# Which tokens of the second layer are put off: a block in four of 32 groups in place of the last 8 groups whole

## The chip, the cores and the metric

The kernel runs on one core of one Trainium2 chip. The metric is device time in microseconds, from runs of the whole kernel; smaller is better. The engines are PE (matmuls; PEld is its load of weights), DVE, ACT and POOL; SP issues transfers.

## The reference, cut to what matters

```
X = fft(fft(x, axis=1), axis=2).real          # 8 x 3072 x 256, as 24576 tokens
h = (X @ w1) * (X @ w2) @ w3                  # 256 -> 1024 -> 1024
y = h @ w_out                                 # 1024 -> 256
logits = y @ w_gate                           # 8 experts
...                                           # greedy routing, 3072 tokens an expert
out[mask] = relu(y[mask] @ w1[e]) @ w2[e]
```

`w3`, `w_out` and `w_gate` are multiplied out ahead, so the second layer is one product with a matrix `W` of 1024 x 264: 256 columns give `y`, the last 8 the logits.

## The kernel before, in words

**Stage A** (`stage_a`, line 280) walks over 8 batches, 2 sets of frequencies and 3 columns of tokens: 48 groups of 512 tokens, numbered 0 to 47. Each group has 8 steps, one for each slice `f` of 128 of the 1024 hidden features; the list `steps` (line 957) has 384 of them, and the loop at line 967 runs it.

A step has a front and a back. `front` (line 813) makes the two first products by 13 matmuls (12 of 256 columns at lines 220 to 222 through `mm3`, one of 512 at line 836). ACT copies one half (840), DVE makes sum, difference (842, 843) and their product `qs` (859), ACT rounds that to float32r as `ah` (853), and POOL makes the rest `al = qs - ah` (854). `back` (line 896) runs three steps later (`LAG = 3`) and multiplies with `W`: `l2` (line 792) takes 4 blocks of 128 tokens, each as the weights of three matmuls of 264 columns (ah with both parts of `W`, then al with the high part), at lines 800, 801 and 804, and at 796 through `mm3` in the last slice. After slice 7, ACT copies the four accumulators, POOL stores logits in `L` and token numbers (`store`, line 915), and SP writes the rows to `xs_d`.

Between steps the loop also folds the input of the next batch on POOL (`fold_batch`, line 456, three loads `xt` of 1 MB a batch) and makes the transforms of the next set (`dft_a`, `dft_b`; the tables of the latter are cut by `tb`, line 316). `middle` (line 921) makes the column that the symmetry leaves over, in the last set of the last batch.

**What is put off.** The last 8 groups (`ASIDE = 8`, line 29; `number` at line 861 counts them 0 to 7) don't run `l2` in stage A. Routing needs every logit, so `logits` (line 876) makes these alone: the 16 columns of the gate in `W`, high and low part side by side (`gates`, line 1003), are the weights, and the 512 tokens move:

```
nc.tensor.matmul(a[:2 * E], gates[0][:, f], ahl[0], start=f == 0, ...)
nc.tensor.matmul(a[:E], gates[0][:, f, :E], ahl[1], start=False, ...)
```

After the last slice ACT copies the 16 rows, four matmuls turn them (line 890) and DVE puts them in `L` (894). `ah` and `al` of seven of these groups go to `away` in DRAM by SP (856, 857); those of the last one (`KEPT = 1`) are written straight to the places of two tables that are done with (`put`, line 868).

**Stage B** (`stage_b`, line 1018) routes the tokens and runs the experts. Its first routing is a chain of small operations that leaves PE idle; the generator `putoff` (line 1334) fills those gaps with the second layer of the tokens put off: 8 lots of 8 slices, 12 matmuls of 256 columns each (line 1371).

**Order.** PE, DVE, ACT and POOL run in the order that the program writes (`manual_schedule(engines=ALL)`, `ALL` on line 203 names these four; SP's order is not written by hand). `later(n, fn)` and `due()` put a piece n steps off.

Of the kernel before, what the change touches and what calls it, by code (L numbers as in the profile page):

```python
# [224 lines left out]
@with_exitstack  # L225
def body(ctx, tc, I, out, nb=NB, dbg=None):
    nc = tc.nc
    vec, act, pool = nc.vector, nc.scalar, nc.gpsimd
    dram = ctx.enter_context(tc.tile_pool(name="dram", bufs=1, space=bass.MemoryType.DRAM))
    xs_d = dram.tile([N, XW], F32, name="xs_d")  # L230
    ed = dram.tile([2, NB, 3, 768], F32R, name="ed")
    em = dram.tile([3, NB], F32R, name="em")
    sp_d = dram.tile([8, NB, 128], F32R, name="sp_d")
    md = dram.tile([NB, D], F32, name="md")
    away = dram.tile([max(ASIDE - KEPT, 1), NF, 128, 2, 512], F32R, name="away")

    keep = ctx.enter_context(tc.tile_pool(name="keep", bufs=1))
    own = ctx.enter_context(tc.tile_pool(name="own", bufs=1))
    L = keep.tile([128, E, NT], F32, name="L")
    small = keep.tile([128, SMALL.shape[1]], F32, name="small")  # L240
    sc = {k: small[:, o:o + w] for k, (o, w) in SOFF.items()}

    aside = 0 if dbg else ASIDE
    putoff = {}
    if dbg == "A":
        nc.vector.memset(L, 0.0)
    if dbg == "B":
        nc.sync.dma_start(L, I["Lin"])
        nc.sync.dma_start(small, I["small"])
        xs_d = I["xs"]  # L250
        k = loader(K_ns(locals()))
    else:
        k = loader(K_ns(locals()))
        stage_a(tc, I, nb, k)
    if dbg == "A":
        nt = 24 * nb
        nc.sync.dma_start(out["L"], L)
        nc.sync.dma_start(out["xs"][:nt * 128], xs_d[:nt * 128])
        return
    stage_b(tc, I, out, k)  # L260
# [19 lines left out]
def stage_a(ctx, tc, I, nb, k):  # L280
# [7 lines left out]
    def accs(i):  # L288
        return psum.tile([128, 512], F32, tag=f"acc{i}", name=f"acc{i}", bufs=1)
# [523 lines left out]
    def front(g):  # L813
        b, st, q, f = g
        c = slice(q * 256, (q + 1) * 256)
        (Eh, El), (Oh, Ol) = EOs[(b, st)]
        if f == 0:
            if g == steps[0]:
                extras(g)
            e3t[0] = e3t[1]  # L820
        if f == 4:
            i = steps.index(g) + 4
            if i < len(steps):
                extras(steps[i])
        e3 = e3t[0]
        n = number(g)
        spill = 0 <= n < k.aside - KEPT

        qs = work.tile([128, 512], F32, name="qs", bufs=4)
        ab = qs.rearrange("p (s c) -> p s c", s=2)  # L830

        us, ue = l1(), l1()
        for w in range(2):
            o = us[:, w * 256:(w + 1) * 256]
            mm3(nc, o, SW[0][:, w, fs(f)], SW[1][:, w, fs(f)], Oh[:, c], Ol[:, c], w == 0, True)
        nc.tensor.matmul(ue, ew[:, fs(f)], e3.rearrange("p w c -> p (w c)"), start=True, stop=False, skip_group_check=True)  # L836
        for w in range(2):
            o = ue[:, w * 256:(w + 1) * 256]
            mm3(nc, o, CW[0][:, w, fs(f)], CW[1][:, w, fs(f)], Eh[:, c], El[:, c], False, True)
        act.activation(qs, us, AF.Copy)  # L840
        pm = work.tile([128, 2, 2, 256], F32, name="pm", bufs=1)
        vec.tensor_tensor(pm[:, 0].rearrange("p w c -> p (w c)"), ue, qs, op=ALU.add)  # L842
        vec.tensor_tensor(pm[:, 1].rearrange("p w c -> p (w c)"), ue, qs, op=ALU.subtract)  # L843
        if n < 0 or spill:
            ah = work.tile([128, 512], F32R, name="ah", bufs=3)
            al = work.tile([128, 512], F32R, name="al", bufs=3)
        else:
            ah, al = put(f)
        if n >= 0:
            k.putoff[n, f] = None if spill else (ah, al)  # L850

        def parts():
            act.activation(ah, qs, AF.Copy)  # L853
            (vec if n == k.aside - 1 and f in LAST else pool).tensor_tensor(al, qs, ah, op=ALU.subtract)  # L854
            if spill:
                cp(nc.sync, k.away[n, f, :, 0], ah)
                cp(nc.sync, k.away[n, f, :, 1], al)

        return ah, al, parts, lambda: vec.tensor_tensor(ab, pm[:, :, 0], pm[:, :, 1], op=ALU.mult)  # L859

# [7 lines left out]
    def put(f):  # L868

        key, t = (("tabA", tabA), ("tabB", tabs["B"]))[f // 4]  # L870
        if key not in places:
            places[key] = own.tile(list(t.shape), F32R, name=key).rearrange("p a b -> p (a b)")
        at = f % 4 * 1024
        return places[key][:, at:at + 512], places[key][:, at + 512:at + 1024]

    def logits(n, f, ahl, j0):

        if f == 0:
            acct[0] = accs(n % 4)
        a = acct[0]  # L880
        nc.tensor.matmul(a[:2 * E], gates[0][:, f], ahl[0], start=f == 0, stop=False, skip_group_check=True)
        nc.tensor.matmul(a[:E], gates[0][:, f, :E], ahl[1], start=False, stop=f == NF - 1, skip_group_check=True)
        if f < NF - 1:
            return
        lt = work.tile([2 * E, 512], F32, name="xo")
        u = accs((n + 2) % 4)[:, :4 * E].rearrange("p (i e) -> p i e", i=4)

        def turn():
            for i in range(4):
                nc.tensor.matmul(u[:, i], lt[:, i * 128:(i + 1) * 128], sc["twice"][:2 * E], start=i == 0, stop=i == 3, skip_group_check=True)  # L890

        later(1, lambda: act.activation(lt, a[:2 * E], AF.Copy))
        later(2, turn)
        later(3, lambda: vec.tensor_copy(L[:, :, j0:j0 + 4].rearrange("p e j -> p j e"), u))

    def back(g, ahl):
        b, st, q, f = g
        n = number(g)
        if n >= 0:
            logits(n, f, ahl, (b * 6 + st * 3 + q) * 4)  # L900
            return
        if f == 0:
            acct[0] = [accs(i) for i in range(4)]
        acc = acct[0]
        l2(acc, ahl[0], ahl[1], f, 4)
        if f < NF - 1:
            return
        j0 = (b * 6 + st * 3 + q) * 4
        for h in range(2):
            xo = work.tile([128, 2, 264], F32, name="xo")  # L910
            act.activation(xo[:, 0], acc[2 * h][:, :264], AF.Copy)
            (vec.tensor_copy(xo[:, 1], acc[2 * h + 1][:, :264]) if EV else act.activation(xo[:, 1], acc[2 * h + 1][:, :264], AF.Copy))
            later(1, lambda xo=xo, j=j0 + 2 * h: store(xo, j))

    def store(xo, j):
        pool.tensor_copy(L[:, :, j:j + 2].rearrange("p e j -> p j e"), xo[:, :, D:])
        pool.tensor_copy(xo[:, :, D:D + 4], sc["tok"][:, j:j + 2, None].to_broadcast([128, 2, 4]))
        nc.sync.dma_start(k.xs_d[j * 128:(j + 2) * 128].rearrange("(i p) d -> p i d", p=128), xo[:, :, :XW])


    def middle():
# [25 lines left out]
        for b in range(nb):  # L947
            p, j = DUP[b]
            if b == nb - 1:
                yield  # L950
            nc.sync.dma_start(L[p:p + 1, :, j], xo[b:b + 1, D:])
            if j // 4 < nb * 6 - k.aside:
                nc.sync.dma_start(k.xs_d[j * 128 + p:j * 128 + p + 1, :D], xo[b:b + 1, :D])
        yield

# [62 lines left out]
def stage_b(ctx, tc, I, out, k):  # L1018
# [315 lines left out]
    def putoff():  # L1334
# [11 lines left out]
            ready.append(k.putoff[n, f])  # L1346

        def finish(n, acc):
            j0 = NT - 4 * ASIDE + 4 * n
            for i in range(2):  # L1350
                xo = ex.tile([128, 2, XW], F32, name="xo")
                act.activation(xo[:, :, :D], acc[i], AF.Copy)
                j = j0 + 2 * i
                pool.tensor_copy(xo[:, :, D:], k.sc["tok"][:, j:j + 2, None].to_broadcast([128, 2, 4]))
                nc.sync.dma_start(xrows[j * 128:(j + 2) * 128].rearrange("(i p) d -> p i d", p=128), xo)
            for b, (p, j) in enumerate(DUP):
                if j0 <= j < j0 + 4:
# [58 lines left out]
    def later(n, fn):  # L1416
        late.append([n, fn])
# [228 lines left out]
```

## Time and profile before

| | us |
|---|---|
| median of 3 runs | 2814.88 (2814.3 to 2817.58) |
| the profiled execution | 2810.5 |
| its span, first to last instruction | 2808.7 |
| PE busy | 2674.4 (95%) |
| DVE, POOL, ACT busy | 2135.4, 1518.0, 1323.0 |

The profile is of one execution. Its time of 2810.5 us lies 4.4 below the median of the runs; the span within it is 1.8 shorter. Busy times are those of one engine each and overlap. Matmuls are pipelined: a matmul's duration is longer than the time to the next one's start, and it is the latter that adds up.

### The profile page before, as it was taken

The numbers are of one execution on the slowest core, as the hardware profiler recorded it, in microseconds if no ns is written. First come the engines' busy times: TensorE is split into PE (matmuls) and PEld (weight loads), VectorE is DVE, ScalarE is ACT, GpSimd is POOL, SyncE is SP. The second block draws the span as 40 slices with busy tenths as digits, with TensorE's granted clock in tenths as the row PEclk, the third lists the DMA queues.
The fourth block names the chain that finished last, engine by engine and source line by source line (L and its number), as shares of the span: only waits on it lengthen the run. The fifth ranks groups of instructions, "written<-read, shape, count | busy, mean of one in ns | idle before, by whom it ended". The sixth has DMA issues, their size and how long they took to land.

```text
span 2808.7 us, 51817 instructions
## 1 busy us (share of the span) xinstructions
PE 2674.4 (95%) x19903; PEld 2454.0 (87%) x19903; DVE 2135.4 (76%) x3795; ACT 1323.0 (47%) x2383; POOL 1518.0 (54%) x1529
## 2 busy tenths in 40 slices
PE   4999999999999999999996999989999999999998
PEld 2899999999999999987796788878888888889997
DVE  8788787978878797888877888788787878862222
ACT  2344444444444444444363747466573746543332
POOL 7295775939577593964304244353535435363532
PEclk8999999999999999999997999999999999999999
DMA  6410110101011011145394112211212122121211
GB/s 232 133 54 32 39 46 24 54 32 54 32 39 47 24 52 34 52 162 200 128 338 154 36 65 54 69 50 46 76 43 73 48 67 54 43 68 43 76 46 35
DMA packets 104705, 207.32 MB, mean 74 GB/s; under 512 B 35178, under 2 KB 60442, under 8 KB 99338
## 3 DMA queue, kind: packets, MB, share of 16 engines
q1 hardware_dynamic: 81000, 131.02, 13.7%
q0 software_dynamic: 22224, 72.58, 8.0%
q8 instruction: 157, 2.57, 0.4%
q14 instruction: 90, 0.74, 0.1%
q10 hardware_dynamic: 1234, 0.41, 0.1%
HBM read 118.15 MB, written 80.28 MB: 71 GB/s over the span
## 4 chain that ended last, share of the span: by engine, by line
PE 73%; DVE 17%; ACT 3%; issue 2%; DMA 1%; POOL 1%; another core or an unknown queue 0%; DVEq 0%; ACTq 0%; POOLq 0%; SPq 0%
PE yp L1483 13%; PE l L220 7%; PE l L222 7%; PE l L221 7%; PE acc L804 5%; PE acc L800 5%; PE acc L801 5%; PE hp L220 4%; PE hp L221 4%; PE hp L222 4%; DVE oR L1086 4%; PE l L836 3%; DVE W L1466 2%; ACT ja L1081 2%; PE hp L1371 2%
## 5 line engine op out<-in xcount | busy, mean ns | idle before, releaser
L854 POOL TENSOR_TENSOR al<-qs,ah 128x512 fp32r<-128x512 f32 x376 | 513.4, 1365 | 406.2 <-ACT ah L853 311.4
L1483 PE MATMUL yp<-FA,W 128*128 128x256 f32 x3040 | 622.0, 286 | 17.8 <-DVE W L1466 8.4
L1483 PEld LDWEIGHTS yp<-FA,W 128*128 128x128 f32 x3040 | 497.8, 190 | 44.6 <-ACT yo L1489 14.9
L859 DVE TENSOR_TENSOR qs<-pm 128x512 f32<-128x512 f32 x384 | 427.4, 1113 | 41.2 <-DVE pm L843 1.8
L853 ACT ACTIVATE ah<-qs 128x512 fp32r<-128x512 f32 x376 | 237.2, 631 | 358.2 <-DVE qs L859 317.7
L1466 DVE SCALAR_TENSOR_TENSOR W<-hp,W 128x512 fp32r<-128x512 f32 x336 | 230.1, 687 | 227.0 <-ACT W L1462 205.0
L1483 PE MATMUL yp<-FB,W 128*128 128x256 f32 x1520 | 388.0, 282 | 0.0
L842 DVE TENSOR_TENSOR pm<-l,qs 128x512 f32<-128x512 f32 x384 | 264.7, 689 | 149.4 <-PE l L222 116.2
L840 ACT ACTIVATE qs<-l 128x512 f32<-128x512 f32 x384 | 227.0, 591 | 235.3 <-PE l L222 220.0
L220 PE MATMUL hp<-tabA,tabB 128*128 128x512 f32 x768 | 319.5, 416 | 0.9 <-ACT tabA L1432 0.9
L1493 POOL DMA_INDIRECT out_dram<-yo,oi x188 | 191.7, 1020 | 231.3 <-DMA out_dram<-yo,oi 217.8
L1462 ACT ACTIVATE W<-hp 128x512 fp32r<-128x512 f32 x336 | 197.2, 593 | 251.6 <-PE hp L222 232.7
L221 PE MATMUL hp<-tabA,tabB 128*128 128x512 f32 x768 | 304.0, 396 | 6.0 <-DVE tabA L1436 6.0
L1483 PEld LDWEIGHTS yp<-FB,W 128*128 128x128 f32 x1520 | 287.9, 189 | 14.3
L800 PE MATMUL acc<-W,ah 128*128 128x264 f32 x1120 | 283.6, 284 | 0.0
L801 PE MATMUL acc<-W,ah 128*128 128x264 f32 x1120 | 283.3, 284 | 0.0
L1086 DVE TENSOR_SCALAR_CACHE_REDUCE oR<-oR,nx 128x1536 uint16<-128x1536 uint16 x196 | 281.4, 1459 | 0.0
L843 DVE TENSOR_TENSOR pm<-l,qs 128x512 f32<-128x512 f32 x384 | 261.2, 680 | 0.0
L1407 POOL DMA_INDIRECT xt<-xs_d,idx x192 | 194.9, 1015 | 109.1 <-issue 49.9
L1457 POOL TENSOR_TENSOR W<-xo,W 128x512 fp32r<-128x512 f32 x48 | 66.6, 1387 | 336.8 <-ACT W L1455 321.1
L222 PE MATMUL hp<-tabA,tabB 128*128 128x512 f32 x624 | 246.7, 395 | 0.0
L220 PE MATMUL l<-eo,SW 128*128 128x256 f32 x768 | 220.7, 287 | 0.0
(350 smaller groups left out, 6930.4 us busy)
## 6 DMA issues: line engine op xcount, KB each, us to landing
xs_d<-xo SPq DMA_DIRECT2D x96, 260.0 KB
xt<-in_xg_dram SPq DMA_DIRECT2D x24, 1024.0 KB
away<-ah SPq DMA_DIRECT2D x56, 256.0 KB
away<-al SPq DMA_DIRECT2D x56, 256.0 KB
yo<-away SPq DMA_DIRECT2D x28, 512.0 KB
raw<-in_w3t_dram SPq DMA_DIRECT2D x16, 512.0 KB
FA<-away SPq DMA_DIRECT2D x14, 512.0 KB
FB<-away SPq DMA_DIRECT2D x14, 512.0 KB
```

The lines of the kernel that those rows point to most:

```text
L220: nc.tensor.matmul(out, ah, bh, start=start, stop=False, skip_group_check=True)
L221: nc.tensor.matmul(out, ah, bl, start=False, stop=False, skip_group_check=True)
L222: nc.tensor.matmul(out, al, bh, start=False, stop=stop, skip_group_check=True)
L800: nc.tensor.matmul(acc[i][:, :264], ah[:, a], W[0][:, f], start=f == 0, stop=False, skip_group_check=True)
L801: nc.tensor.matmul(acc[i][:, :264], ah[:, a], W[1][:, f], start=False, stop=False, skip_group_check=True)
L842: vec.tensor_tensor(pm[:, 0].rearrange("p w c -> p (w c)"), ue, qs, op=ALU.add)
L843: vec.tensor_tensor(pm[:, 1].rearrange("p w c -> p (w c)"), ue, qs, op=ALU.subtract)
L854: (vec if n == k.aside - 1 and f in LAST else pool).tensor_tensor(al, qs, ah, op=ALU.subtract)
L859: return ah, al, parts, lambda: vec.tensor_tensor(ab, pm[:, :, 0], pm[:, :, 1], op=ALU.mult)
L1086: vec.tensor_scalar(jk[:, :n], T[:, :n], nx[:, i:i + 1], None, op0=ALU.is_ge, op1=ALU.add, accum_out=acc[:, i:i + 1])
L1466: vec.scalar_tensor_tensor(hl, hp, 0.0, hh, op0=ALU.max, op1=ALU.subtract)
L1483: nc.tensor.matmul(yp[i], hhl[seq[s][0]][:, t[i]], seq[s][1], start=f == 0 and s == 0 and (i % 2 == 0 or len(yp) == 4), stop=f == NF - 1 a ...
```

## The change

Instead of 8 whole groups, 32 groups (16 to 47) each put off one of their four blocks of 128 tokens, the last one. `ASIDE` becomes 32 and a new `PUT = 8` counts the lots for stage B; a lot holds the fourth blocks of four groups, so its shape is the old one. In these groups `back` calls `l2` for three blocks and `logits` for the fourth: two matmuls of 128 columns into the fourth accumulator. The turn after the last slice is one matmul, its rows lie in a buffer of `qs`, its result in one of `l1`, and ACT copies it to `L`. `ah` and `al` are always the working tiles; SP copies their last 128 columns to `away`, or, for the last lot, to the places of the tables. `store` writes one or two blocks; the accumulators are all copied by ACT, as before (`EV` was 0). In stage B, `finish` writes its rows to every fourth block.

```
-ASIDE, KEPT = 8, 1
+PUT, KEPT = 8, 1
+ASIDE = 4 * PUT
...
-        if n < 0 or spill:
-            ah = work.tile([128, 512], F32R, name="ah", bufs=3)
-            al = work.tile([128, 512], F32R, name="al", bufs=3)
-        else:
-            ah, al = put(f)
+        ah = work.tile([128, 512], F32R, name="ah", bufs=3)
+        al = work.tile([128, 512], F32R, name="al", bufs=3)
         if n >= 0:
-            k.putoff[n, f] = None if spill else (ah, al)
+            k.putoff[m, f] = None if m < PUT - KEPT else put(f)
+            away = [k.away[m, f, :, h, side] for h in range(2)] if m < PUT - KEPT else [t[:, side] for t in put(f)]
...
-            if spill:
-                cp(nc.sync, k.away[n, f, :, 0], ah)
-                cp(nc.sync, k.away[n, f, :, 1], al)
+            if n >= 0:
+                cp(nc.sync, away[0], ah[:, 384:])
+                cp(nc.sync, away[1], al[:, 384:])
...
-    def logits(n, f, ahl, j0):
+    def logits(a, f, ahl, j):
...
-        nc.tensor.matmul(a[:2 * E], gates[0][:, f], ahl[0], start=f == 0, stop=False, skip_group_check=True)
-        nc.tensor.matmul(a[:E], gates[0][:, f, :E], ahl[1], start=False, stop=f == NF - 1, skip_group_check=True)
+        nc.tensor.matmul(a[:2 * E, :128], gates[0][:, f], ahl[0][:, 384:], start=f == 0, stop=False, skip_group_check=True)
+        nc.tensor.matmul(a[:E, :128], gates[0][:, f, :E], ahl[1][:, 384:], start=False, stop=f == NF - 1, skip_group_check=True)
...
-        n = number(g)
-        if n >= 0:
-            logits(n, f, ahl, (b * 6 + st * 3 + q) * 4)
-            return
+        n = 3 if number(g) >= 0 else 4
+        j0 = (b * 6 + st * 3 + q) * 4
...
-        l2(acc, ahl[0], ahl[1], f, 4)
+        l2(acc, ahl[0], ahl[1], f, n)
+        if n < 4:
+            logits(acc[3], f, ahl, j0 + 3)
```

## Rows read from the trace of the kernel before

**Rows 1.** The page: PE and DVE over the span, then PE and its clock by slices.
```profile
PE 2674.4 (95%) x19903; PEld 2454.0 (87%) x19903; DVE 2135.4 (76%) x3795; ACT 1323.0 (47%) x2383; POOL 1518.0 (54%) x1529
...
PE   4999999999999999999996999989999999999998
...
PEclk8999999999999999999997999999999999999999
```

**Rows 2.** Windows: stretch, its length, busy PE, PEld, DVE, ACT, POOL, clock, DMA, GB/s.
```profile
988.00:1152.10 164.10, 164.06 (x1288) 160.34 (x1287) 134.73 (x175) 71.84 (x138) 113.72 (x113) 1.00 0.12 40
1202.50:1385.30 182.80, 174.28 (x1176) 145.21 (x1174) 159.41 (x226) 85.37 (x156) 88.01 (x75) 1.00 0.48 177
1385.30:1394.70 9.40, 4.94 (x15) 2.27 (x14) 5.59 (x15) 3.48 (x5) 2.52 (x3) 0.60 0.00 0
...
988.00:1012.90 24.90, 24.90 (x202) 24.56 (x201) 23.40 (x26) 11.44 (x22) 24.49 (x24) 1.00 0.19 65
1012.90:1038.50 25.60, 25.56 (x203) 24.79 (x202) 23.83 (x28) 11.57 (x23) 25.40 (x25) 1.00 0.19 63
1038.50:1065.00 26.50, 26.50 (x211) 26.15 (x210) 24.46 (x37) 12.48 (x24) 18.18 (x20) 1.00 0.18 62
1065.00:1094.70 29.70, 29.70 (x229) 29.35 (x228) 20.83 (x30) 12.25 (x23) 10.58 (x12) 1.00 0.06 19
1094.70:1125.30 30.60, 30.60 (x239) 29.31 (x238) 22.16 (x32) 11.98 (x23) 12.52 (x14) 1.00 0.06 19
1125.30:1152.10 26.80, 26.80 (x215) 26.18 (x214) 20.05 (x26) 12.13 (x24) 22.55 (x23) 1.00 0.07 22
```

**Rows 3.** Timeline, group 31 into 32: start, duration, engine, line, operation.
```profile
984.90 0.39 PE L836 MATMUL l<-e,ew 128*128 128x512 f32 x1
...
985.83 0.29 PE L800 MATMUL acc<-W,ah 128*128 128x264 f32 x1
...
987.28 0.28 PE L220 MATMUL l<-eo,SW 128*128 128x256 f32 x1
...
988.00 0.40 PE L836 MATMUL l<-e,ew 128*128 128x512 f32 x1
```

**Rows 4.** Timeline of PE, group 44, one step's logits and the next matmul.
```profile
1298.40 0.40 PE L881 MATMUL acc<-ah,gates 128*16 128x512 f32 x1
1298.63 0.40 PE L882 MATMUL acc<-al,gates 128*8 128x512 f32 x1
1298.87 0.27 PE L220 MATMUL l<-eo,SW 128*128 128x256 f32 x1
```

**Rows 5.** Groups of DVE's instructions, 1202.5 to 1385.3: busy us, mean ns, idle before.
```profile
L859 DVE TENSOR_TENSOR qs<-pm 128x512 f32<-128x512 f32 x63 | 62.8, 996 | 6.9 <-POOL al L854 0.5
L842 DVE TENSOR_TENSOR pm<-l,qs 128x512 f32<-128x512 f32 x64 | 44.2, 690 | 12.9 <-PE l L222 6.8 <-ACT qs L840 1.1
L843 DVE TENSOR_TENSOR pm<-l,qs 128x512 f32<-128x512 f32 x64 | 43.5, 680 | 0.0
```

**Rows 6.** PE's instructions of `middle` by form, whole span: one row of each kind.
```profile
L220 PE MATMUL l<-W,ah 128*8 128x264 f32 x8 | 2.3, 283 | 0.0
...
L220 PE MATMUL l<-CW,mbe 128*8 128x512 f32 x4 | 1.6, 400 | 0.0
```

**Rows 7.** Timeline of PE in the expert stage: first of three short matmuls, second wide one.
```profile
1590.02 0.17 PE L1179 MATMUL rps<-cnt,blk 128*128 128x4 f32 x1
...
1590.48 0.28 PE L1483 MATMUL yp<-FB,W 128*128 128x256 f32 x1
```

**Rows 8.** Line 663, plain float32: duration min/median/max in ns, first and last start.
```profile
L663 PE MATMUL acc<-tabB,xt x128: 383/386/806, 68.3 to 110.0; 128*128 128x264 f32 x128
```

**Rows 9.** Timeline of PE: six records of line 663 in a row.
```profile
97.72 1.50 PE L663 MATMUL acc<-tabB,xt 128*128 128x264 f32 x6
```

**Rows 10.** Timeline of SP, group 40: one issue of a transfer put off.
```profile
1213.05 0.32 SPq L216 DMA_DIRECT2D away<-ah  x1
```

**Rows 11.** Waits of SP, whole span: us in total, times, longest us.
```profile
SPq L471 <- POOL FO L374: 93.7, 13, 9.7
```

**Rows 12.** Windows, 993 to 995, while one `xt` is loaded (columns as in rows 2).
```profile
993.00:995.00 2.00, 2.00 (x18) 1.96 (x17) 1.76 (x4) 1.14 (x2) 2.00 (x2) 1.00 0.89 369
```

More of the change, by code (lines that the diff above doesn't have):

```diff
@@ L234, in body @@
     md = dram.tile([NB, D], F32, name="md")
-    away = dram.tile([max(ASIDE - KEPT, 1), NF, 128, 2, 512], F32R, name="away")
+    away = dram.tile([max(PUT - KEPT, 1), NF, 128, 2, 512], F32R, name="away")
     keep = ctx.enter_context(tc.tile_pool(name="keep", bufs=1))
@@ L826, in front @@
         n = number(g)
-        spill = 0 <= n < k.aside - KEPT
+        m, side = n // 4, slice(n % 4 * 128, n % 4 * 128 + 128)
         qs = work.tile([128, 512], F32, name="qs", bufs=4)
@@ L874, in put, with lower_rows @@
         return places[key][:, at:at + 512], places[key][:, at + 512:at + 1024]
-    def logits(n, f, ahl, j0):
-        if f == 0:
-            acct[0] = accs(n % 4)
-        a = acct[0]
-        nc.tensor.matmul(a[:2 * E], gates[0][:, f], ahl[0], start=f == 0, stop=False, skip_group_check=True)
-        nc.tensor.matmul(a[:E], gates[0][:, f, :E], ahl[1], start=False, stop=f == NF - 1, skip_group_check=True)
+    def logits(a, f, ahl, j):
+        nc.tensor.matmul(a[:2 * E, :128], gates[0][:, f], ahl[0][:, 384:], start=f == 0, stop=False, skip_group_check=True)
+        nc.tensor.matmul(a[:E, :128], gates[0][:, f, :E], ahl[1][:, 384:], start=False, stop=f == NF - 1, skip_group_check=True)
         if f < NF - 1:
             return
-        lt = work.tile([2 * E, 512], F32, name="xo")
-        u = accs((n + 2) % 4)[:, :4 * E].rearrange("p (i e) -> p i e", i=4)
+        u = []
+        def lower_rows():
+            u.append(work.tile([2 * E, 128], F32, name="qs", bufs=4))
+            act.activation(u[0], a[:2 * E, :128], AF.Copy)
         def turn():
-            for i in range(4):
-                nc.tensor.matmul(u[:, i], lt[:, i * 128:(i + 1) * 128], sc["twice"][:2 * E], start=i == 0, stop=i == 3, skip_group_check=True)
-        later(1, lambda: act.activation(lt, a[:2 * E], AF.Copy))
+            lt, u[0] = u[0], l1()[:, :E]
+            nc.tensor.matmul(u[0], lt, sc["twice"][:2 * E], start=True, stop=True, skip_group_check=True)
+        later(1, lower_rows)
         later(2, turn)
-        later(3, lambda: vec.tensor_copy(L[:, :, j0:j0 + 4].rearrange("p e j -> p j e"), u))
+        later(3, lambda: act.activation(L[:, :, j], u[0], AF.Copy))
     def back(g, ahl):
         b, st, q, f = g
-        n = number(g)
-        if n >= 0:
-            logits(n, f, ahl, (b * 6 + st * 3 + q) * 4)
-            return
+        n = 3 if number(g) >= 0 else 4
+        j0 = (b * 6 + st * 3 + q) * 4
         if f == 0:
@@ L904, in back @@
         acc = acct[0]
-        l2(acc, ahl[0], ahl[1], f, 4)
+        l2(acc, ahl[0], ahl[1], f, n)
+        if n < 4:
+            logits(acc[3], f, ahl, j0 + 3)
         if f < NF - 1:
             return
-        j0 = (b * 6 + st * 3 + q) * 4
         for h in range(2):
             xo = work.tile([128, 2, 264], F32, name="xo")
-            act.activation(xo[:, 0], acc[2 * h][:, :264], AF.Copy)
-            (vec.tensor_copy(xo[:, 1], acc[2 * h + 1][:, :264]) if EV else act.activation(xo[:, 1], acc[2 * h + 1][:, :264], AF.Copy))
-            later(1, lambda xo=xo, j=j0 + 2 * h: store(xo, j))
+            for i in range(min(n - 2 * h, 2)):
+                act.activation(xo[:, i], acc[2 * h + i][:, :264], AF.Copy)
+            later(1, lambda xo=xo[:, :min(n - 2 * h, 2)], j=j0 + 2 * h: store(xo, j))
     def store(xo, j):
-        pool.tensor_copy(L[:, :, j:j + 2].rearrange("p e j -> p j e"), xo[:, :, D:])
-        pool.tensor_copy(xo[:, :, D:D + 4], sc["tok"][:, j:j + 2, None].to_broadcast([128, 2, 4]))
-        nc.sync.dma_start(k.xs_d[j * 128:(j + 2) * 128].rearrange("(i p) d -> p i d", p=128), xo[:, :, :XW])
+        n = xo.shape[1]
+        pool.tensor_copy(L[:, :, j:j + n].rearrange("p e j -> p j e"), xo[:, :, D:])
+        pool.tensor_copy(xo[:, :, D:D + 4], sc["tok"][:, j:j + n, None].to_broadcast([128, n, 4]))
+        nc.sync.dma_start(k.xs_d[j * 128:(j + n) * 128].rearrange("(i p) d -> p i d", p=128), xo[:, :, :XW])
     def middle():
@@ L951, in middle @@
             nc.sync.dma_start(L[p:p + 1, :, j], xo[b:b + 1, D:])
-            if j // 4 < nb * 6 - k.aside:
+            if j // 4 < nb * 6 - k.aside or j % 4 < 3:
                 nc.sync.dma_start(k.xs_d[j * 128 + p:j * 128 + p + 1, :D], xo[b:b + 1, :D])
@@ L1348, in finish @@
         def finish(n, acc):
-            j0 = NT - 4 * ASIDE + 4 * n
+            g0 = NT // 4 - ASIDE + 4 * n
+            rows = xrows.rearrange("(g a p) d -> p g a d", a=4, p=128)
             for i in range(2):
@@ L1352, in finish @@
                 act.activation(xo[:, :, :D], acc[i], AF.Copy)
-                j = j0 + 2 * i
-                pool.tensor_copy(xo[:, :, D:], k.sc["tok"][:, j:j + 2, None].to_broadcast([128, 2, 4]))
-                nc.sync.dma_start(xrows[j * 128:(j + 2) * 128].rearrange("(i p) d -> p i d", p=128), xo)
+                g = g0 + 2 * i
+                pool.tensor_copy(xo[:, :, D:], k.sc["tok"][:, 4 * g + 3:4 * g + 8:4, None].to_broadcast([128, 2, 4]))
+                nc.sync.dma_start(rows[:, g:g + 2, 3], xo)
             for b, (p, j) in enumerate(DUP):
-                if j0 <= j < j0 + 4:
+                if g0 <= j // 4 < g0 + 4 and j % 4 == 3:
                     nc.sync.dma_start(xrows[j * 128 + p:j * 128 + p + 1, :D], k.md[b:b + 1])
```

## The prediction

> **What bounds the kernel now.** I read the page first: the span is 2808.7 us, PE is busy for 95% of it and its row of slices is full but for the start and a few slices in the middle, while its clock is at the full 2.4 GHz in most of them; DVE comes next with 76% [rows 1]. The windows by group of 512 tokens come next, cut at the first L836 matmul of a group. One batch of six groups (988.0 to 1152.1) takes 164.1 us; PE works in 164.06 of them, DVE in 134.73, POOL in 113.72 [rows 2]. PE sets the pace there: a step, from one L836 to the next, takes 3.11 us [rows 3]. The twelve matmuls of the second layer run from 985.83 to 987.28, 1.45 us or 0.121 each [rows 3], so the thirteen of the front take 1.66. Only the two groups in which most of the next batch is folded come near a second limit: POOL is busy for 24.49 of 24.90 and 25.40 of 25.60 us [rows 2]. The second of them has the plain length of 24.9 plus some 0.6, lost to POOL.
>
> The last eight groups, put off whole, look different. A step there needs 1.66 us of front and two matmuls of 512 columns, 0.23 and 0.24 us [rows 4]: 2.13 us. DVE's three operations of a step cost 0.69 + 0.68 + 1.00 = 2.37 us [rows 5], more than PE's step. What that lost can be summed: with the whole second layer these groups would take 26.5, 29.7, 30.6 and 26.8 us for those places in a batch [rows 2], four times the plain 24.9 (nothing is folded or transformed for a batch after the last), and the column work of `middle`, 16 matmuls of 512 columns and 24 of 264 [rows 6] (twelve and four at L927 and L928, eight times three at L942), some 16 x 0.235 + 24 x 0.121 = 6.7 us, and 0.8 for eight small ones. That is 220.7. They take 182.8 [rows 2], so 37.9 us were saved where 64 x (1.45 - 0.47) = 62.7 us of PE work were taken out; 24.8 were lost. PE's own work would now fill 220.7 - 62.7 = 158.0 us and DVE's fills 159.41 [rows 2]; two engines with about equal loads, bound step by step through the ring of accumulators, wait for each other in turn.
>
> **The change part by part.** The part put off keeps its size: eight lots of 8 x 12 matmuls at L1371, spread over 32 groups instead of 8. So the routing stage is costed at nothing; the last kept slices land by DMA after the last groups, and seven lots of twelve matmuls run before the last one is wanted.
>
> *Removed in each of 256 steps:* three matmuls, 3 x 0.121 = 0.363 us.
>
> *Added in each:* two float32r matmuls of 128 columns, the gate columns as weights. This is the step that decides, and no row shows a float32r product of more than 4 and fewer than 256 columns. From below: at one pass a column costs 0.235 / 512 = 0.46 ns [rows 4], so 0.059 us. The next front matmul must load 128 columns of weights, and a matmul too short to hide such a load is charged for it: three matmuls of 4 columns (L1179, L1101, L1102) and the wide one after them take from 1590.02 to 1590.48 [rows 7], which leaves 0.113 for each short one. So the pair costs 0.059 + 0.113 = 0.172 at least. From above: plain float32 at L663 takes two records a matmul (128 for 64 [rows 8]), and six records of 264 columns take 1.50 us [rows 9]; less the last one's 0.386 [rows 8] that is 0.223 each, 0.446 a matmul, 1.69 ns a column, four times the one-pass rate. 128 columns: 0.216, the pair 0.432. I take the upper end. The operands are 4-byte words; every one-pass row has a moving side of at least 256 columns, and the tables of the second transform, with 192 or 193 columns in use, are read 256 wide (`tb`, line 319), which leaves the traces silent on just the width that the change uses. The nearest one-pass row below is of 4 columns, where any rate hides under the load of the weights. That is a reading, not a row, and so it gets a little over half the chance. The Trainium skill (FP8 and Floating Point Precision, "TensorE Precision Notes") gives true FP32 four passes through the array, as L663's two records at twice the time agree, and its reduced form a single read, with no width below which that is lost; by it the pair would have the lower price, which is rival 1.
>
> So a step changes by 0.432 - 0.363 = +0.069 us.
>
> *Groups 16 to 39* (24 of them, whole before): 192 x 0.069 = +13.2. In the longer step POOL's shortage of 0.6 in one group of each of four batches goes: -2.4.
>
> *Groups 40 to 47:* 220.7 + 64 x 0.069 = 225.1 in place of 182.8: +42.3. This term is known best: those groups get three of four blocks of their second layer back, and the fourth's logits at the slow price.
>
> *The end of stage A:* 9.4 us now, with PE at work for 4.94 [rows 2]. Three more steps of nine matmuls go in, 3.3 us, and hide in that idle time except the last, 1.1; DVE is less behind when it begins. I take 0, from -2 to +3.
>
> *The turn:* 32 times one block instead of 8 times four: 64 records either way, no change. Its extra turns in the rings of `l1` and `qs` take one buffer of four for about a step; the former holder is over a step old by then, so nothing. The copy to L moves from DVE to ACT, which has slack (71.84 of 164.1 [rows 2]).
>
> *DMAs:* 112 of 256 KB become 512 of 64 KB. SP issues one in 0.32 us [rows 10], so 0.64 of each 3.2 us step; traffic drops from the 177 GB/s of those groups [rows 2] to about a quarter, spread out. I take 0; the cover is the ring of three `ah` and `al` buffers, priced in rival 3.
>
> *Sum:* 13.2 - 2.4 + 42.3 = +53.1, on a profiled execution of 2810.5 us (span 2808.7). The median of the runs, 2814.88, stands 4.4 above it; so about **2868**. If the four-fold price follows 512 one-pass columns (0.235 each) instead, 256 x 0.038 = 9.7 more: 2878. The case's own range is 2860 to 2886.
>
> **Rivals.**
> 1. *One pass at any width, not slower.* The pair costs 0.172, a step falls by 0.191. Groups 16 to 39 gain 36.7, but the two folding groups can't fall below POOL's 24.49 + 25.40 = 49.9 [rows 2]: they give 0.6 of 3.1, so 2.5 are lost in each of four batches, leaving 26.7. The last eight take 220.7 - 12.2 = 208.5, or 25.7 more than now. Net -1: 2814, from 2804 (POOL's work shifts between groups) to 2822. For it: the logits of 512 columns run at one pass with such weights [rows 4]. It decides from a pair price under some 0.2. The Trainium skill (TensorE: Matmul & The Clock Gate, "Back-to-back issue gap") gives about 81 ns for a matmul of 128 columns in a stream of loads and matmuls; the pair would cost 0.162 by it, an estimate that lands here too. Its figure for 512 columns, 131 ns, is well below the 0.235 measured here [rows 4], so it adds no weight.
> 2. *One pass, but each short matmul is charged 0.113* [rows 7]: pair 0.226, step -0.137. Groups 16 to 39: -26.3 and POOL's 1.6 lost four times, -19.9; the last eight +29.1. Net +9: 2824.
> 3. *SP becomes the bound.* Its queue waits in order: 93.7 us over 13 loads of `xt` for POOL, 9.7 at worst [rows 11]. A put-off block behind such a load would wait 9.7 plus the 2.8 us that 1 MB takes at 369 GB/s [rows 12], 12.5 in all, against the 3 x 3.18 = 9.5 us until its buffer is written again: 3.0 us each, for three loads in each of four batches 36 us more: 2904. Against it: the wait is for POOL's own work, and POOL makes `al` behind that work anyway, so the block is seldom ready sooner; and the order on SP isn't written by hand (line 203 leaves it out).
>
> **How the numbers follow.** Forecast 0.55, rival 1 0.30, rival 2 0.10, rival 3 0.05. The range runs from 2811, which takes in most of rival 1, to 2886, the forecast's upper end; it leaves out rival 3 and the low third of rival 1. About 0.2% (5.6 us) is what a measurement can tell from no change. Below 2809 lies about a third of rival 1: faster 0.10. Within 0.2%: half of rival 1, 0.15. The rest, 0.75, is slower.
>
> **What would show it.** In the changed profile the row of L881 and L882 with 128 columns: starts some 0.22 apart mean my price, 0.06 and then 0.11 mean rival 1. Steps of groups 16 to 47 should last 3.18 us (2.92 for rival 1, 2.97 for rival 2) with PE full throughout; the stretch from the first L836 of group 40 to the last of stage A about 225 us, not 183. If `ah` at L853 waits for DMA, rival 3 holds. If the routing stage's own length moves by more than 3 us, the claim that it stays as it was is wrong. The forecast fails if the pair of narrow matmuls costs less than three matmuls of 264 columns.

## The result, and the profile after

The changed kernel takes 2833.35 us, the median of 4 runs (2830.93 to 2835.22), against 2814.59 for the kernel before on the same chip (4 runs, 2813.24 to 2817.58): +18.8 us, a ratio of 1.0068 with a 95% interval of 1.0055 to 1.0082. It is slower, as forecast, but by a third of the forecast's +53, and for other reasons.

The profiled execution took 2835.22 us, span 2833.1. That is 24.7 us more than the profiled execution of before; of this, 4.1 + 1.9 is only where the two lie against these medians (2810.5 below 2814.59, 2835.22 above 2833.35). Lines stand a little apart in the changed kernel: L836 is now L837, L881 and L882 are L877 and L878, L220 to L222 are L221 to L223, `al` is L853. The page, answering to [rows 1]:

```profile
PE 2693.0 (95%) x20287; PEld 2480.3 (88%) x20287; DVE 2109.8 (74%) x3787; ACT 1328.1 (47%) x2439; POOL 1522.4 (54%) x1561
```

PE is as full as it was and has 18.6 us more to do (2674.4 before); the share says nothing of what became of the step. The timeline does. PE in a plain step of the changed kernel (start, duration, engine, line, operation), answering to [rows 3] and [rows 4]:

```profile
1285.50 0.40 PE L837 MATMUL l<-e,ew 128*128 128x512 f32 x1
...
1287.53 0.22 PE L877 MATMUL acc<-ah,gates 128*16 128x128 f32 x1
1287.59 0.22 PE L878 MATMUL acc<-al,gates 128*8 128x128 f32 x1
1287.65 0.33 PE L221 MATMUL l<-eo,SW 128*128 128x256 f32 x1
1287.82 0.27 PE L222 MATMUL l<-eo,SW 128*128 128x256 f32 x1
...
1288.41 0.39 PE L837 MATMUL l<-e,ew 128*128 128x512 f32 x1
```

The step lasts 2.91 us, as rival 1 had it (2.92). The two narrow matmuls take 0.06 us each by their starts, and the wide one behind them 0.17 instead of its usual 0.12. PEld starts to load the wide one's weights with the second narrow matmul, at 1287.59, and the next weights at 1287.70; of these 0.11 us the narrow matmul covers only 0.06. So the pair costs 0.06 + 0.06 + 0.05 = 0.17 us. That is rival 1's price (0.172) to the digit, and not the 0.432 of the forecast: float32r runs at one pass with 128 columns too.

The stages come next, cut at the first L836 or L837 of group 16, at that of group 40, at the last one of stage A, at the first reduce of the routing (`v<-L`), and at the first gather of the experts' tokens (`xt<-xs_d`). The windows of the kernel before (columns as in [rows 2]):

```profile
546.30:1202.50 656.20, 656.05 (x5142) 641.18 (x5141) 537.68 (x697) 286.41 (x543) 454.75 (x449) 1.00 0.12 40
1202.50:1383.20 180.70, 172.53 (x1166) 144.15 (x1165) 157.48 (x223) 84.52 (x154) 87.26 (x74) 1.00 0.48 179
```

The same windows of the changed kernel, and the end of stage A:

```profile
547.30:1187.60 640.30, 633.03 (x4999) 606.95 (x4998) 521.52 (x698) 283.77 (x564) 456.30 (x449) 1.00 0.24 75
1187.60:1397.50 209.90, 209.68 (x1664) 198.58 (x1663) 151.28 (x220) 91.34 (x183) 95.17 (x103) 1.00 0.22 67
1397.50:1404.90 7.40, 6.62 (x56) 6.15 (x54) 3.84 (x13) 4.59 (x9) 2.02 (x5) 1.00 0.16 45
```

The reduce and the gather by their first and last start (line, operation, count: duration in ns, minimum, median and maximum, first and last start), kernel before:

```profile
L1127 DVE TENSOR_REDUCE v<-L x7: 2782/2986/2995, 1394.8 to 2319.9; 128x192 f32<-128x1536 f32 x7
L1407 POOL DMA_INDIRECT xt<-xs_d,idx x192: 942/960/2302, 1514.5 to 2746.2; - x192
```

And in the changed kernel:

```profile
L1126 DVE TENSOR_REDUCE v<-L x7: 2780/2984/2990, 1404.9 to 2345.0; 128x192 f32<-128x1536 f32 x7
L1407 POOL DMA_INDIRECT xt<-xs_d,idx x192: 942/960/2302, 1534.6 to 2771.0; - x192
```

| stretch | before | after | change | rival 1 | forecast |
|---|---|---|---|---|---|
| start to group 16 | 546.3 | 547.3 | +1.0 | 0 | 0 |
| groups 16 to 39 | 656.2 | 640.3 | -15.9 | -26.7 | +10.8 |
| group 40 to the last front | 180.7 | 209.9 | +29.2 | +25.7 | +42.3 |
| last front to first reduce | 11.6 | 7.4 | -4.2 | 0 | 0 |
| first reduce to first gather | 119.7 | 129.7 | +10.0 | 0 | 0 |
| first gather to end of span | 1294.2 | 1298.5 | +4.3 | 0 | 0 |

The stretches are cut where the last front begins, one step ahead of the prediction's cut (1385.3 in the kernel before), so that step lies in the fourth row and not in the third. The last row is scatter: the changed kernel with another turn (turn_rows, below) differs from it in nothing behind the first gather and takes 2822.9 - 1530.5 = 1292.4 there; on other chips this stretch takes 1287.9 in a variant of the kernel before (before_f125) and 1289.4 in one of the changed kernel (dup_turn). So what is to be explained is some +10 in stage A, where rival 1's price would give -1, and +10 in the routing, where everybody had nothing.

**Stage A.** Rival 1 is off by 10.8 us in its first 24 groups and by 3.5 in the last eight. Most of this is one step in each group. PE in the step that holds the turn of the changed kernel:

```profile
1282.13 0.39 PE L837 MATMUL l<-e,ew 128*128 128x512 f32 x1
...
1284.16 0.22 PE L877 MATMUL acc<-ah,gates 128*16 128x128 f32 x1
1284.22 0.22 PE L878 MATMUL acc<-al,gates 128*8 128x128 f32 x1
1284.37 0.38 PE L889 MATMUL l<-small,qs 16*128 16x8 f32 x2
1284.68 0.39 PE L221 MATMUL l<-eo,SW 128*128 128x256 f32 x1
1284.90 0.29 PE L222 MATMUL l<-eo,SW 128*128 128x256 f32 x1
...
1285.50 0.40 PE L837 MATMUL l<-e,ew 128*128 128x512 f32 x1
```

The step lasts 3.37 us; the plain one right behind it 2.91. From L878 to the start of L222 it is 0.68 us here and 0.23 in the plain step: the two records of 8 columns cost 0.45. They take 0.31 themselves, L878 ahead of them 0.15 instead of 0.06, and L221 behind them 0.22 instead of 0.17. What sets the turn apart is its 16 contracted rows ("16*128") between matmuls of 128. The kernel before shows such a change of rows too, where 64 follow on 128 in `dft_b`:

```profile
303.10 0.28 PE L222 MATMUL l<-tabB,FB 128*128 128x256 f32 x1
303.31 0.38 PE L220 MATMUL l<-tabB,FB 64*128 64x256 f32 x1
303.53 0.28 PE L221 MATMUL l<-tabB,FB 64*128 64x256 f32 x1
```

The starts are 0.21 and 0.22 us apart here, not 0.12, and the same on the way back to 128 rows (304.00, 304.21, 304.43): one change of rows costs some 0.19 us. Before, the 8 groups with turns were those where DVE took longer for a step than PE.

In the last eight groups 8 x 0.45 = 3.6 is what is missing (3.5). In the first 24, 24 x 0.45 would be 10.8 too, but that it fits is luck: in 8 of these groups POOL sets the pace, and there a turn on PE costs next to nothing (turn_rows, below). These are the two groups of each batch in which most of the folding falls. In the changed kernel, groups 32 and 33:

```profile
976.80:1001.50 24.70, 24.39 (x196) 23.26 (x195) 23.27 (x26) 11.43 (x23) 24.31 (x25) 1.00 0.33 102
1001.50:1027.50 26.00, 24.66 (x197) 23.35 (x196) 22.53 (x29) 12.18 (x24) 25.80 (x24) 1.00 0.31 96
```

POOL is busy for 24.31 of 24.70 and 25.80 of 26.00 us; PE alone would need 8 x 2.92 + 0.45 = 23.8 for each. Together they take 50.7 us, 0.2 more than before (24.9 + 25.6 [rows 2]), where rival 1 had them fall to 49.9. That is 0.8 a batch, 3.2 in four batches; with the turns of the other groups, 16 x 0.45 = 7.2, it makes 10.4 of the 10.8. What PE waits for most between 550 and 1400 us (us in total, times, longest):

```profile
PE acc L805 <- POOL al L853: 5.0, 12, 0.6
```

**Routing.** PE fills the gaps of the routing with what was put off, and is full there. The window of the kernel before from 40 us behind the first reduce, 20 us long:

```profile
1434.70:1454.70 20.00, 19.85 (x166) 19.43 (x165) 16.32 (x39) 14.62 (x23) 0.38 (x2) 1.00 1.03 375
```

The same window of the changed kernel:

```profile
1444.90:1464.90 20.00, 18.36 (x147) 17.51 (x147) 13.87 (x34) 11.91 (x18) 0.38 (x2) 1.00 0.94 332
```

PE now falls short by 1.5 us in 20 (by 1.9 in the next 20), and the transfers by a tenth. Both kernels move the same put-off data. The waits of SP in the routing (us in total, times, longest) show what differs. Kernel before:

```profile
SPq L1358 <- DMA xs_d<-xo: 6.6, 2, 4.1
```

Changed kernel:

```profile
SPq L1358 <- DMA xs_d<-xo: 29.8, 6, 7.2
```

L1358 writes the row of a token of the leftover column (`md`) over a row that the store of its lot (L1355) has just written, so it has to wait until that store has landed. Each of the 8 batches has one such token. Before, two of the eight lay in the last 8 groups; now six lie in a fourth block of the last 32. SP's queue goes in order, and behind five of the six stand loads for the lots to come. The timeline of SP after (start, duration, line, transfer):

```profile
1428.86 0.88 SPq L1355 DMA_DIRECT2D xs_d<-xo  x2
1429.83 0.42 SPq L217 DMA_DIRECT2D yo<-away  x1
1437.01 0.52 SPq L1358 DMA_DIRECT2D xs_d<-md  x1
1437.62 0.53 SPq L217 DMA_DIRECT2D FA<-away  x1
```

From 1430.25 to 1437.01 SP issues nothing, and the loads of `away` behind it start that much later. These two readings, the turn's rows and SP's queue, were then tried one by one.

### The profile page after: what moved, and what is told of

The parts are those of the page before. It is cut to its first block, busy times and chain, and to the rows that moved or that the text cites. A ratio compares the mean times of both kernels' runs of the same rounds, so it can differ in the third digit from the quotient of the medians.

```text
span 2833.1 us, 53523 instructions
## 1 busy us (share of the span) xinstructions
PE 2693.0 (95%) x20287; PEld 2480.3 (88%) x20287; DVE 2109.8 (74%) x3787; ACT 1328.1 (47%) x2439; POOL 1522.4 (54%) x1561
## 4 chain that ended last, share of the span: by engine, by line
PE 69%; DVE 15%; POOL 5%; issue 4%; DMA 3%; ACT 3%; another core or an unknown queue 0%; SPq 0%; POOLq 0%; ACTq 0%; DVEq 0%
PE yp L1483 13%; PE l L221 8%; PE l L223 7%; PE l L222 7%; PE hp L221 4%; PE acc L805 4%; PE hp L222 4%; PE hp L223 4%; PE acc L801 4%; PE acc L802 4%; DVE oR L1085 4%; PE l L837 3%; DVE W L1466 2%; POOL al L853 2%; ACT ja L1080 2%
## 5 line engine op out<-in xcount | busy, mean ns | idle before, releaser
L853 POOL TENSOR_TENSOR al<-qs,ah 128x512 fp32r<-128x512 f32 x383 | 525.1, 1371 | 416.5 <-ACT ah L852 312.0
L858 DVE TENSOR_TENSOR qs<-pm 128x512 f32<-128x512 f32 x384 | 403.9, 1052 | 38.4 <-DVE pm L844 0.9
L221 PE MATMUL hp<-tabA,tabB 128*128 128x512 f32 x768 | 320.9, 418 | 0.9 <-ACT tabA L1432 0.9
L222 PE MATMUL hp<-tabA,tabB 128*128 128x512 f32 x768 | 305.1, 397 | 5.9 <-DVE tabA L1436 5.9
L223 PE MATMUL hp<-tabA,tabB 128*128 128x512 f32 x624 | 247.1, 396 | 0.0
L221 PE MATMUL l<-eo,SW 128*128 128x256 f32 x768 | 232.8, 303 | 0.0
```

The costliest lines, as they stand in the source:

```text
L221: nc.tensor.matmul(out, ah, bh, start=start, stop=False, skip_group_check=True)
L222: nc.tensor.matmul(out, ah, bl, start=False, stop=False, skip_group_check=True)
L223: nc.tensor.matmul(out, al, bh, start=False, stop=stop, skip_group_check=True)
```

## The experiments

A ratio is always to the kernel before, run on the same chip beside the variant. The first four and the changed kernel ran on chips where before takes 2814.5; on the chips of the others it takes 2803.6 to 2803.7, so ratios are compared, not times.

**1. The rows of the leftover column written last (dup_last).** They are collected and issued behind all lots.

```diff
-                    nc.sync.dma_start(xrows[j * 128 + p:j * 128 + p + 1, :D], k.md[b:b + 1])
+                    fix.append(lambda p=p, j=j, b=b: nc.sync.dma_start(xrows[j * 128 + p:j * 128 + p + 1, :D], k.md[b:b + 1]))
...
-        for fn in after:
+        for fn in after + fix:
```

> The changed kernel, but the rows of the leftover column (line 1358) are written to xs_d after all lots of put-off work, not behind each lot. Theory (SP stands behind each of these writes until the lot's store has landed, and the loads of put-off data queue behind it): the routing stage, from the first reduce of v to the first gather, falls from 129.7 us to about 120, the time from 2833 to 2823 to 2826. Rival (the stage is longer for another reason, such as stores that reach every fourth block): within 3 us of 2833, the stage still about 130.

Measured: 2821.90 (10 runs), ratio 1.0029 (1.0019 to 1.0040), 11.5 us below the changed kernel. First reduce and first gather:

```profile
L1126 DVE TENSOR_REDUCE v<-L x7: 2790/2991/2996, 1403.7 to 2328.1; 128x192 f32<-128x1536 f32 x7
...
L1407 POOL DMA_INDIRECT xt<-xs_d,idx x192: 942/961/2300, 1520.5 to 2755.6; - x192
```

116.8 us between them (129.7 in the changed kernel, 119.7 before). The same stretch as above, 40 us behind the reduce:

```profile
1443.70:1463.70 20.00, 19.85 (x167) 19.56 (x166) 16.35 (x43) 13.60 (x22) 0.76 (x4) 1.00 1.01 354
```

PE is at 19.85 again. The +10 in the routing is the order on SP's queue: with another order it is gone. That the stage is even 2.9 us shorter than before need not be a gain of the change: the kernel before has two such writes itself, with 6.6 us of waits, and wasn't run with them last.

**2. The turn with all 128 rows (turn_rows).** The 16 rows stand in a tile of 128 that ACT has zeroed, and the whole of `twice` is its partner; the sums are the same.

```diff
-            u.append(work.tile([2 * E, 128], F32, name="qs", bufs=4))
-            act.activation(u[0], a[:2 * E, :128], AF.Copy)
+            u.append(work.tile([128, 128], F32, name="qs", bufs=4))
+            act.activation(u[0], sc["ident"], AF.Copy, scale=0.0)
+            act.activation(u[0][:2 * E], a[:2 * E, :128], AF.Copy)
...
-            nc.tensor.matmul(u[0], lt, sc["twice"][:2 * E], start=True, stop=True, skip_group_check=True)
+            nc.tensor.matmul(u[0], lt, sc["twice"], start=True, stop=True, skip_group_check=True)
```

> The changed kernel, but the turn of the 16 logit rows contracts over 128 rows (the other 112 zero, written by ACT) instead of 16. Theory (of the 0.45 us that a turn adds to its step, half is for going to a matmul of 16 rows and back): the step with the turn falls from 3.37 to about 3.14 us, 32 times 0.23, the time from 2833 to about 2826. Rival (the 0.45 us are two loads of 128 columns of weights and waits for ACT): the step stays at 3.37 or more, the time at 2833.

Measured: 2827.92 (4 runs), ratio 1.0052 (1.0032 to 1.0071), 5.4 us below the changed kernel. PE in a step with the turn:

```profile
1302.21 0.39 PE L837 MATMUL l<-e,ew 128*128 128x512 f32 x1
...
1304.29 0.22 PE L878 MATMUL acc<-al,gates 128*8 128x128 f32 x1
1304.35 0.34 PE L890 MATMUL l<-small,qs 128*128 128x8 f32 x2
1304.54 0.37 PE L221 MATMUL l<-eo,SW 128*128 128x256 f32 x1
...
1305.34 0.39 PE L837 MATMUL l<-e,ew 128*128 128x512 f32 x1
```

The step is 3.13 us instead of 3.37, with the same columns moved: half of the turn's price was its rows. PEld shows what the rows change. The load of the turn's weights in the changed kernel, and here:

```profile
1284.37 0.29 PEld L889 LDWEIGHTS l<-small,qs 16*128 16x128 f32 x2
1304.29 0.30 PEld L890 LDWEIGHTS l<-small,qs 128*128 128x128 f32 x2
```

With 16 rows it begins with the turn's own matmul (1284.37); with 128, 0.06 us ahead of it, beside L878 (1304.29). Of 32 x 0.24 = 7.7 us, 5.4 came through. The two folding groups of the same batch as above show why not more:

```profile
974.60:999.40 24.80, 24.24 (x196) 23.19 (x195) 23.33 (x26) 11.85 (x24) 24.40 (x25) 1.00 0.33 102
999.40:1025.40 26.00, 24.44 (x197) 23.27 (x196) 22.53 (x29) 12.37 (x25) 25.80 (x24) 1.00 0.31 96
```

They take 24.8 and 26.0 us, against 24.7 and 26.0 in the changed kernel: in the 8 folding groups POOL takes what PE saves, which leaves 24 x 0.24 = 5.8.

**3. The fold spread over more steps (fold115).** POOL's pieces for the next batch begin three steps earlier and come more thinly.

```diff
-    LAG, FOLD, EV, AH, W8 = 3, 1.3, 0, 1, 1
-    FOLD_AT = 3
+    LAG, FOLD, EV, AH, W8 = 3, 1.15, 0, 1, 1
+    FOLD_AT = 0
```

> The changed kernel, but the fold of the next batch begins three steps earlier and runs at 1.15 units a step instead of 1.3, so the same POOL work is spread over more steps. Theory (POOL bounds the steps of the folding groups): groups 20 to 22 take 24 + 24 + 25.3 us instead of 24.7 + 26.0 + 25.9, about 3 us less in each of four batches, the time from 2833 to 2821 to 2825. Rival (these steps stall because the transfers of al and ah hold their buffers): no change beyond 3 us, 2830 to 2836.

Measured: 2829.26 (4 runs), ratio 1.0057 (1.0037 to 1.0077), 4.1 below the changed kernel. The windows of three groups of another batch, which take 24.7, 26.0 and 25.8 in the changed kernel:

```profile
656.50:680.30 23.80, 23.80 (x196) 23.12 (x195) 21.53 (x28) 11.90 (x23) 23.49 (x22) 1.00 0.27 88
680.30:704.10 23.80, 23.80 (x197) 23.12 (x196) 19.80 (x25) 11.48 (x23) 23.68 (x23) 1.00 0.35 107
704.10:731.50 27.40, 26.02 (x206) 24.68 (x205) 23.90 (x36) 12.25 (x25) 17.93 (x20) 1.00 0.32 98
```

PE's longest wait in stage A (us in total, times, longest):

```profile
PE l L223 <- DVE FA L380: 6.6, 5, 1.4
```

The first two fell to the 23.8 that PE alone needs: POOL was what held them. But the fold now ends late, and PE waits for its last part, `FA`, 1.4 us in each batch. Half right: the limit is real, and so is the deadline behind it.

**4. A third narrow matmul, with 128 columns of weights (wide_weights).** It is marked as a new start (`start=True`) in the bank of the logits, and the kernel's output differs from that of the changed kernel, so where tokens go may differ too. The amount of work is the same but for the matmul added: first reduce to first gather takes 130.1 us, 129.7 in the changed kernel.

```diff
+        nc.tensor.matmul(a[:, 128:256], W[0][:, f, :128], ahl[0][:, 384:], start=True, stop=True, skip_group_check=True)
```

> The changed kernel with one more float32r matmul in each of the 256 steps: 128 columns moving, 128 columns of W as weights, into columns that nobody reads, between the last matmul of 264 columns and the logits. Theory (128 columns move at one pass whatever the weights, and the load hides under the matmul before): +0.059 us a step, 256 times, the time 2833 + 15 = 2848, a little less where POOL sets the pace. Rival (one pass at 128 columns only with narrow weights, four passes with wide ones): +0.216 us a step, 2833 + 55 = 2888.

Measured: 2843.82 (4 runs), ratio 1.0111 (1.0089 to 1.0133), 10.5 above the changed kernel. PE at the end of a step's second layer:

```profile
851.76 0.22 PE L877 MATMUL acc<-ah,W 128*128 128x128 f32 x1
851.82 0.22 PE L878 MATMUL acc<-ah,gates 128*16 128x128 f32 x1
851.88 0.22 PE L879 MATMUL acc<-al,gates 128*8 128x128 f32 x1
851.94 0.33 PE L221 MATMUL l<-eo,SW 128*128 128x256 f32 x1
```

0.06 for each. So a product of 128 columns takes one pass with 128 columns of weights as with 8 or 16. 256 x 0.06 = 15.4 us of PE work cost 10.5: a batch of six groups went from 160.2 to 162.1 us, 1.9 for 48 x 0.06 = 2.9, the rest lying in the groups that wait for POOL.

**5. Both repairs (dup_turn), and the fold moved as well (all3_f125, all3_f120; before_f125 is the kernel before with the same fold as all3_f125).** For all3_f120:

```diff
-    LAG, FOLD, EV, AH, W8 = 3, 1.3, 0, 1, 1
-    FOLD_AT = 3
+    LAG, FOLD, EV, AH, W8 = 3, 1.2, 0, 1, 1
+    FOLD_AT = 2
...
-                fg, credit = fold_batch(b + 1, F, 2), -4 * FOLD
+                fg, credit = fold_batch(b + 1, F, 2), -2 * FOLD
```

all3_f125 and before_f125 have 1.25, 1 and -3 in these places.

> The changed kernel with both edits, the writes of the leftover rows last and the turn over 128 rows. Theory (they act in different stages and add): 2833.4 - 11.5 - 5.4 = 2816.5, within 3. Rival (the shorter steps with a turn are given back to POOL or to the routing stage): 2820 or more.

> Both edits and the fold from one step after the set's start, first work three steps later, at 1.25 units a step: it ends some two steps sooner than at 1.15, so the transform at step 14 should no longer wait for it (in fold115 it cost 1.9 us a batch in groups 22, 28, 34 and 40). Theory (POOL's bound and that wait are all that is left of the folding groups): 2816.5 less 7 to 11, 2806 to 2810, faster than the kernel before. Rival (at 1.25 POOL is over its capacity again): 2812 to 2817.

> As all3_f125, but the fold starts one step later and runs at 1.2 units a step, so it ends about one step later. If the wait of the transform is the larger loss, slower than all3_f125 by 2 to 5 us; if POOL's capacity is, faster by as much. Expected 2806 to 2812.

> The kernel before with the same spread of the fold alone. Its steps of 3.11 us leave POOL only 0.6 us short in one group of each of six batches: theory -2 to -4 us, 2811 to 2813. If it gains as much as the changed kernel does (7 or more), the folding groups' loss does not come from the shorter step.

| kernel | median us (runs) | ratio | interval |
|---|---|---|---|
| dup_turn | 2808.42 (10) | 1.0014 | 1.0005 to 1.0024 |
| all3_f125 | 2807.75 (11) | 1.0014 | 1.0005 to 1.0023 |
| all3_f120 | 2802.87 (11) | 0.9997 | 0.9988 to 1.0006 |
| before_f125 | 2802.78 (10) | 0.9995 | 0.9986 to 1.0005 |

The repairs add up: 1.0068 - 0.0039 - 0.0016 = 1.0013. The fold at 1.25 gives nothing to either kernel; at 1.2 it gives 5.5 us, and the changed kernel with all three edits is level with the one before. It doesn't beat it, and the kernel before was not run with its own late writes issued last, nor with the fold at 1.2.

**6. The last of the fold given one or two steps more (s23, s34), and a ninth and tenth lot put off (s23_p9, s23_p10),** all on all3_f120. In these four, `rows` is not put off along with the splits: the row that it loads into `FB` is issued at 639.8 us in s23, ahead of the split of the first third (663.1), which then writes over it; in all3_f120 the load comes at 665.1, behind that split. So part of the folded input is wrong; the amount of work is the same.

```diff
-            later(wait + (3 if t == 2 else 1) if wait else 0, ...
-            later(wait + (4 if t == 2 else 2) if wait else 0, ...
+            later(wait + (3 if t == 2 else 2) if wait else 0, ...
+            later(wait + (4 if t == 2 else 3) if wait else 0, ...
```

s34 has 3 and 4 there; s23_p9 and s23_p10 have `PUT, KEPT = 9, 1` and `10, 1`.

> As all3_f120, with the splits of the first two folded thirds put off one step more (DVE takes them 4 and 5 steps behind the fold's end on POOL instead of 3 and 4). In all3_f120 group 25 loses 0.8 us at one step and group 26 1.2 at another, where DVE stands behind such a split that POOL has not fed yet. Theory: both stalls go, some 2 us less in each of four batches, 5 to 8 us under all3_f120: 0.2 to 0.3% faster than the kernel before. Rival (the stalls are POOL's own lag and only move): as all3_f120, within 0.1% of the kernel before.

> As s23 with one step more still (5 and 6 steps). If s23 removes the stalls, the same time as s23 within 2 us; if POOL lags by more than a step, a further 2 to 5 us.

> As s23 with nine lots put off instead of eight: four more groups (12 to 15) give up a block. Stage A loses 32 steps times 0.19 less four turns of 0.23, 5.2 us; the routing stage gets 96 more matmuls of 0.118 (11.3 us) and 4 MB more to load. Theory (the put-off work ends some 20 us before the first index is there, so the added lot still fits): 3 to 5 us under s23. Rival (transfers, nearly always busy there, or PE bound the stage): the routing stage grows by 5 to 11 us, 0 to 6 us over s23.

> As s23_p9 with ten lots (36 + 4 groups, from group 8). Two lots more are 22.6 us of PE work in the routing stage, more than the 20 us left at its end: theory 0 to 5 us over s23_p9, the routing stage longer by 5 to 15 us than in s23.

| kernel | median us (runs) | ratio | interval | reduce to gather, us |
|---|---|---|---|---|
| s23 | 2801.41 (11) | 0.9993 | 0.9984 to 1.0002 | 1511.2 - 1394.2 = 117.0 |
| s34 | 2807.56 (11) | 1.0014 | 1.0005 to 1.0023 | 1518.5 - 1398.9 = 119.6 |
| s23_p9 | 2808.20 (11) | 1.0016 | 1.0007 to 1.0025 | 1517.5 - 1390.8 = 126.7 |
| s23_p10 | 2815.04 (5) | 1.0037 | 1.0024 to 1.0051 | 1523.9 - 1385.9 = 138.0 |

s23 gains nothing that can be told from zero, and s34 loses. A ninth lot takes 3.4 us from stage A (the first reduce starts at 1390.8, not 1394.2) and adds 9.7 to the routing. The whole routing stage of s23 as one window:

```profile
1394.20:1511.20 117.00, 104.38 (x1002) 102.68 (x1002) 92.85 (x245) 61.67 (x102) 9.97 (x23) 0.97 0.83 299
```

And of s23_p9:

```profile
1390.80:1517.50 126.70, 116.45 (x1098) 114.62 (x1098) 91.09 (x245) 62.52 (x104) 10.60 (x25) 0.97 0.87 313
```

96 matmuls more, PE 12.1 us more busy, 9.7 us longer: a lot beyond eight is paid for nearly in full in the routing, while stage A gives back only what the logits and POOL leave of it. Both runs came out slower than even the worse of what was expected of them (6.8 us over s23, and 6.8 over s23_p9). Whether PE or the transfers (0.83 and 0.87 of the DMA engines' time) bound the stage was not told apart.

## Why the prediction was right or wrong

**The side was right by luck; the step that carried it was wrong.** "I take the upper end": the pair of narrow matmuls at 0.432 us. It measured 0.17, less than the three matmuls of 264 columns that it replaces (0.363), which is the prediction's own sign that the forecast fails. At that price the prediction's sum is -1; that the time went up all the same came from terms that it had put at nothing. The prediction held that one pass wasn't shown below 256 columns and gave four passes a little over half. The lower bound was built right from rows (0.059 for a pass, 0.113 for a short matmul ahead of a wide load) and is the measured price; the mistake was to read a gap in the rows as a hint of a cliff. Every float32r row that shows a rate, at 256 columns and more, had one pass, and only another type (L663, plain float32, two records) had four. The Trainium skill (FP8 and Floating Point Precision, "TensorE Precision Notes") names four passes for true FP32 and none for its reduced form, which is read as 4-byte words and truncated; the trace agrees at 128 columns, with 0.06 us. In TensorE: Matmul & The Clock Gate, "Back-to-back issue gap", the Trainium skill gives N / 2.4 + 2.5 ns for matmuls measured alone, some 56 for 128 columns, and some 81 for a stream with loads; here the starts are 0.06 us apart, near the first, and the load shows once, in the 0.05 of the wide matmul behind.

**Groups 40 to 47, "the term known best": +42.3.** Measured +29.2. Its frame held (three of four blocks come back, DVE no longer limits); with 0.172 for the pair it is +25.7, and the turns make it 29.3.

**Groups 16 to 39.** Forecast +10.8, rival 1 -26.7, measured -15.9. That a batch loses time to POOL, as rival 1 had it, is borne out: PE's own work in a batch, turns and all, would be 164.06 - 0.6 - 48 x 0.191 + 6 x 0.45 = 157.0, and it lasts 160.2. The size was a little low: the two folding groups take 50.7 us a batch and not 49.9. The rest is the turn.

**"The turn: 64 records either way, no change."** This failed, by 24 x 0.45 = 10.8 us. The count was right, and a count was not enough: 24 of the 32 turns now stand in groups where PE sets the pace, and each costs 0.45 us there with its neighbours, though its two records move 8 columns each. turn_rows showed that about half of it is due to its 16 rows. The trace of the kernel before held the sign, in the 0.21 and 0.22 us where 64 rows follow on 128.

**"So the routing stage is costed at nothing."** This failed, by +10.0 us, and by the prediction's own mark (a move of over 3 us). The reason given, the same lots of the same size, was true, and dup_last showed that the stage is no longer with them (116.8 against 119.7). What wasn't looked at is which *rows* of `xs_d` belong to them: four more fix-ups, which hold up the loads behind them on SP.

**The end of stage A: 0, from -2 to +3.** Measured -4.2. PE has the second layer of the last steps, three blocks each, to do there and is busy for 6.62 of 7.40 us, at a granted clock of 1.00; before, it was busy for 4.94 of the last 9.40, and these ran at 0.60 [rows 2], between the two levels of 1.2 and 2.4 GHz. Which part the shorter chain on DVE has in this wasn't tried.

**The DMAs at 0, and rival 3.** Held: what PE waits for between 550 and 1400 us is POOL's `al`, DVE's `pm` and nothing of a transfer. SP did become a bound, though, in the other stage and by another wait.

**Rival 2** (0.113 for each short matmul) fell: 0.06 between the two, the load is charged once. So rival 1's sum, the turn, the folding groups, the end of stage A and the routing give -1 + 10.8 + 3.2 - 4.2 + 10.0 = +18.8; measured +18.8 between the medians, closer than runs that lie 4 us apart can be trusted to.

## What to carry to other kernels

When work is put off, follow its stores as well as its matmuls: a small write that must wait for a large one holds up everything behind it on an in-order queue, so issue such fix-ups last (11.5 us here). When an operation moves, ask what bounds the place it moves *to*: a turn costed at nothing took 0.45 us in a step that PE sets and next to nothing in one that POOL sets, and filling up its contracted rows with zeros got half of that back. And a bound worked out from rows is to be taken before a cliff that no row shows.

## What the runs showed of the hardware that was not expected

- Float32r matmuls of 128 columns run at one pass, 0.06 us from start to start, with 8, 16 or 128 columns of weights.
- A plain float32 matmul of 16 contracted rows between matmuls of 128 costs about 0.24 us more than the same with 128 rows (step 3.37 against 3.13), and the matmul ahead of it and the one behind it bear part of that. The load of its weights begins with its own matmul and not beside the one ahead.
- From float32r matmuls of 128 contracted rows to matmuls of 64, and back, the two starts at the change are 0.21 and 0.22 us apart instead of 0.12.
- A row of 256 float32 written over one that a transfer has just stored had SP wait for 5.0 us on average (29.8 over 6), 7.2 at worst.
